# Sink scores in three column tiles, and sink values as a block diagonal

## The chip, the cores and the metric

The kernel runs on one core of one Trainium2 chip. The metric is the time of one execution on the device in microseconds (us); lower is better. Times are medians of several executions. Beside them stands one execution taken with the hardware profiler, from which all rows of the trace come.

## What is computed

Attention with four sink positions and a window of 128, followed by a gated two-layer network:

```python
# q, k, v: 4 batches, 8 heads, 768 positions, 64 wide; n_sink = 4, window = 128
scores = q @ k.transpose(0, 1, 3, 2) / sqrt(64)
rel = pos[:, None] - pos[None, :]
keep = (pos[None, :] < n_sink) | ((rel >= 0) & (rel < window))
a = softmax(where(keep, scores, -1e9))
x = (a @ v).transpose(0, 2, 1, 3).reshape(3072, 512)
# w_in 512 x 2048, w_out 2048 x 512
h = x @ w_in
out = (h * sigmoid(beta * h)) @ w_out
```

All tensors are float32 in memory; the kernel multiplies in bfloat16 and accumulates in float32.

## The kernel before

**Units.** The attention is cut into 32 units. A unit is one batch, one pair of heads and one half of the positions (384 queries); `place(n)` (L441) gives batch, pair, half and buffer. Units 0 to 3 are the first halves of batch 0, 4 to 7 its second halves, and so on, so there are 16 second-half units: 4 to 7, 12 to 15, 20 to 23 and 28 to 31. For each unit q and k are cast to bfloat16 (`cast`, L509, on POOL), turned so that the head dimension lies along the partitions (`transpose_in`, L532, on PE for the first twelve units, a transposing DMA after that), multiplied to scores, sent through the exponential (ACT), masked, multiplied with v (`attend`, L667), divided by the row sums (`normalise`, L702, DVE), and turned back (`transpose_out`, L712) into `xT`, the input of the network.

**Sinks.** Queries of a second half do not see the four sink keys in their window blocks, so these units have a sink part of their own. `sink_keys` (L560, POOL) builds `k_sink`, a 128 by 128 stationary tile that holds the four sink keys of the first head in columns 0 to 3 and of the second head in columns 32 to 35, each zero in the other head's rows; the rest is zero. `scores_sink` (L568) multiplies it with all 384 queries in one matmul (L570) into a bank of PSUM, and one exponential on ACT (L573) writes `E_sink`, 128 by 384. In `attend`, for each of the three blocks of 128 queries, one matmul (L685) multiplies that block of `E_sink` with the unit's part of `v_sink` (130 columns: two heads of 64 values and a one) into the accumulator `av_ps`; the matmuls of the window blocks (L696, 65 columns each) add to it. `v_sink` for all 16 pairs of heads is filled once: `sink_constants` (L428) clears it and sets the ones, two DMAs on ACT's queue (L837) bring the first four rows of v for all heads to `v_rows`, which lies in a part of the buffer `g`, and two casts on DVE (L891) copy them in.

**Pairs of units.** From unit 8 on (`PAIRED`), the scores of two neighbouring units are computed together (`scores_pair`, L620). Scores use the array as two halves of 64 rows, one for each head (L597, L643). The sink scores of a pair's two units are still two matmuls and two exponentials, in the same bank `tr`.

**Network.** `hidden` (L759) multiplies `xT` with w_in in matmuls of 384 columns (L747), `tanh` (L752, ACT) and `gate` (L767, DVE) make `g`, and `project` (L796) multiplies it with w_out in matmuls of 512 columns (L797). The weights come by DMA on SP's queue (`load_w`, L491), in 8 pieces each of w_in and w_out, and are cast by POOL, four of them half by ACT (`cast_w`, L496). Until about 54 us the loads of weights and of q, k and v share the DMA engines.

**Order.** The program is recorded as operations with their reads and writes, in an order set by hand (`EARLY`, `FIRST`, `CASTS`), and `Prog.order` (L182) then lays them on the engines by estimated costs: each engine takes the earliest operation that is ready among the next 160. A node has a flag `tiled`; a change of the flag on PE is reckoned with 97 ns (`CHANGE`). Every engine then runs its list strictly in that order and waits at semaphores.

Of the kernel before, what the change touches and what calls it, by code (L numbers as in the profile page):

```python
# [24 lines left out]
HEAD1 = 32  # L25
# [48 lines left out]
class Node:  # L74
# [5 lines left out]
    def __init__(self, id, eng):  # L80
# [10 lines left out]
        self.tiled = False  # L91


class Prog:
# [39 lines left out]
    def op(self, eng, fn, r=(), w=(), x=(), dma=None, busy=100.0, lag=None, behind=None,  # L134
           give=0.0, line=False, after=None, tiled=False):
# [46 lines left out]
    def order(self):  # L182
# [12 lines left out]
        tiled = False  # L195
# [4 lines left out]
        def best(e):  # L200
# [9 lines left out]
            n = min(c, key=lambda n: (max(n.ready, free[e]) + n.give - self.CHANGE * (tiled and n.tiled), n.id))  # L210
# [97 lines left out]
def bass_streamingllm_window__then__act_swish_beta_kernel(  # L308
# [91 lines left out]
    def constants():  # L400
# [4 lines left out]
        fill("dve", ones[:, :], 1.0, ["ones"], busy=270.0)  # L405
        select(ident[:, :], ones[:, 0:128], [[1, 128]], ALU.is_equal, 0.0, 0, -1, ["ones"], ["ident"])
# [21 lines left out]
    def sink_constants():  # L428
# [131 lines left out]
    def sink_keys(n, after=None):  # L560
        pb = place(n)[3]
        op("gp", lambda e: e.tensor_tensor(
            k_sink[pb][:, 0:2 * HEAD1].rearrange("p (h x) -> p h x", h=2)[:, :, 0:NSINK],
# [4 lines left out]
    def scores_sink(n, bank, name):  # L568
        pb = place(n)[3]
        op("pe", lambda e: e.matmul(bank[:, 0:TT], k_sink[pb][:, :], qkT[pb][:, 1, 0, :],  # L570
                                    start=True, stop=True),
           r=[("k_sink", pb), ("qT", pb, 1)], w=[name], **pe(TT))
        op("act", lambda e: e.activation(E_sink[n % 3][:, :], bank[:, 0:TT], AF.Exp, bias=0.0,  # L573
                                         scale=SCALE),
           x=[name], w=[("E_sink", n % 3)], **act(TT))
# [4 lines left out]
    def scores(n, c, bank, name):  # L580
# [11 lines left out]
        with P.together("pe"):  # L592
            for kb, qb, nq in CHUNKS[half][c]:
                w = 128 * nq
                for hh in range(2):
# [6 lines left out]
                       busy=3.0 + w / 4.8, lag=260.0, tiled=True)  # L602
# [311 lines left out]
    for s in sorted(slots):  # L914
# [16 lines left out]
        for n, step in here:  # L931
# [13 lines left out]
            if step == "av":  # L945
# [107 lines left out]
```

## Time and profile before

| | us |
|---|---|
| median of 3 runs | 222.72 (222.72 to 222.91) |
| profiled execution, its time | 223.15 |
| profiled execution, its span | 221.4 |
| PE busy in the span | 216.1 |
| ACT busy | 145.8 |
| DVE busy | 126.2 |
| POOL busy | 74.0 |

The span reaches from the first to the last instruction; the time has some 1.75 us more around it. PE is TensorE's matmuls, PEld its weight loads, DVE VectorE, ACT ScalarE, POOL GpSimd, SP the queue that issues most DMAs; ACTq is the part of ACT that issues DMAs. Matmuls overlap in the array, so the mean duration of one (327 ns for 384 columns) is longer than the distance between the starts of two; distances are read from groups in the timeline. A busy PE is therefore not the same as a PE at its peak, and the price of a matmul is taken from a dense stretch.

### The profile page before, as it was taken

The numbers are of one execution on the slowest core, as the hardware profiler recorded it, in microseconds if no ns is written. First come the engines' busy times: TensorE is split into PE (matmuls) and PEld (weight loads), VectorE is DVE, ScalarE is ACT, GpSimd is POOL, SyncE is SP. The second block draws the span as 40 slices with busy tenths as digits, with TensorE's granted clock in tenths as the row PEclk, the third lists the DMA queues.
The fourth block names the chain that finished last, engine by engine and source line by source line (L and its number), as shares of the span: only waits on it lengthen the run. The fifth ranks groups of instructions, "written<-read, shape, count | busy, mean of one in ns | idle before, by whom it ended". The sixth has DMA issues, their size and how long they took to land.

```text
span 221.4 us, 4551 instructions
## 1 busy us (share of the span) xinstructions
PE 216.1 (98%) x1765; PEld 123.4 (56%) x1765; DVE 126.2 (57%) x247; ACT 145.8 (66%) x229; POOL 74.0 (33%) x149
## 2 busy tenths in 40 slices
PE   7998999999999999999999999999999999999995
PEld 4554557654555656555465656455656555555543
DVE  5376877773550756665494749484829447074300
ACT  2776997995254868556887778758766675375411
POOL 7697767468625232435012520920000000000000
PEclk9999999999999999999999999999999999999999
DMA  6999999995779994998996989772210202201022
GB/s 192 296 312 345 355 325 266 309 393 146 177 163 236 263 292 117 270 266 134 280 216 140 271 199 224 166 136 60 84 47 18 68 0 83 98 0 47 20 78 96
DMA packets 95438, 39.80 MB, mean 180 GB/s; under 512 B 81960, under 2 KB 88376, under 8 KB 95416
## 3 DMA queue, kind: packets, MB, share of 16 engines
q1 hardware_dynamic: 93760, 38.68, 66.9%
q10 hardware_dynamic: 1656, 0.83, 1.3%
q8 instruction: 14, 0.23, 0.4%
q14 instruction: 8, 0.07, 0.1%
HBM read 27.30 MB, written 6.29 MB: 152 GB/s over the span
## 4 chain that ended last, share of the span: by engine, by line
PE 74%; DMA 11%; SPq 10%; POOL 2%; issue 1%; DVE 0%; POOLq 0%; DVEq 0%
PE acc L797 35%; PE six L747 28%; SPq L467 4%; DMA q_stage<-in_q_dram 4%; SPq L459 4%; PE six L696 4%; PE six L643 4%; DMA wst<-in_moe_w_in_dram 3%; DMA wst<-in_moe_w_out_dram 2%; SPq L493 2%; DMA v_stage<-in_v_dram 1%; PE acc L778 1%; PE six L685 1%; PE six L570 1%; POOL w_out L506 1%
## 5 line engine op out<-in xcount | busy, mean ns | idle before, releaser
L797 PE MATMUL acc<-w_out,g 128*128 128x512 bf16 x368 | 89.2, 379 | 0.2 <-POOL w_out L506 0.2
L755 ACT ACTIVATE th<-six,beta_half 128x384 f32<-128x384 f32 x106 | 61.0, 583 | 26.6 <-PE six L747 21.5
L747 PE MATMUL six<-xT,w_in 128*128 128x384 bf16 x424 | 78.2, 326 | 0.0
L770 DVE SCALAR_TENSOR_TENSOR g<-th,six 128x384 bf16<-128x384 f32 x106 | 57.2, 551 | 25.5 <-ACT th L755 22.9
L747 PEld LDWEIGHTS six<-xT,w_in 128*128 128x128 bf16 x424 | 40.4, 98 | 28.0 <-issue 0.2
L797 PEld LDWEIGHTS acc<-w_out,g 128*128 128x128 bf16 x368 | 34.4, 98 | 37.0 <-issue 1.3
L662 DVE TENSOR_TENSOR E<-E,mask_all 128x1536 bf16<-128x1536 bf16 x24 | 23.9, 998 | 39.6 <-ACT E L654 39.6
L654 ACT ACTIVATE E<-six 128x1536 bf16<-128x1536 f32 x24 | 33.5, 1448 | 15.8 <-PE six L643 15.8
L518 POOL CAST qk<-q_stage 128x384 bf16<-128x384 f32 x32 | 17.6, 552 | 30.1 <-DMA qkT<-qk 15.3
L521 POOL CAST v_aug<-v_stage 128x384 bf16<-128x384 f32 x32 | 17.4, 559 | 18.3 <-DMA v_stage<-in_v_dram 10.9
L805 ACT ACTIVATE out_sb<-acc 128x512 f32<-128x512 f32 x22 | 13.1, 599 | 14.4 <-PE acc L797 14.0
L518 POOL CAST qk<-k_stage 128x384 bf16<-128x384 f32 x31 | 17.4, 564 | 13.0 <-DMA k_stage<-in_k_dram 8.0
L696 PEld LDWEIGHTS six<-v_aug,E 128*128 128x128 bf16 x384 | 17.1, 97 | 3.6 <-DVE E L662 0.3
L696 PE MATMUL six<-v_aug,E 128*128 128x65 bf16 x384 | 18.8, 193 | 0.1
L707 DVE TENSOR_TENSOR o_norm<-six,rden 128x384 bf16<-128x384 f32 x32 | 17.8, 557 | 1.2
L747 PE MATMUL acc<-xT,w_in 128*128 128x384 bf16 x88 | 18.1, 326 | 0.0
L770 DVE SCALAR_TENSOR_TENSOR g<-th,acc 128x384 bf16<-128x384 f32 x22 | 12.0, 551 | 4.0 <-ACT th L755 3.7
L604 ACT ACTIVATE E<-six 128x768 bf16<-128x768 f32 x16 | 12.5, 816 | 2.3 <-PE six L597 2.3
L755 ACT ACTIVATE th<-acc,beta_half 128x384 f32<-128x384 f32 x22 | 12.9, 590 | 1.7 <-PE acc L747 1.4
L747 PEld LDWEIGHTS acc<-xT,w_in 128*128 128x128 bf16 x88 | 7.8, 98 | 4.7 <-DVE g L770 0.4
L643 PEld LDWEIGHTS six<-qkT 64*128 64x128 bf16 x192 | 7.2, 94 | 5.2 <-issue 4.2
L506 POOL CAST w_out<-wst 128x1024 bf16<-128x1024 f32 x8 | 8.3, 1042 | 5.2 <-DMA wst<-in_moe_w_out_dram 5.2
(68 smaller groups left out, 139.2 us busy)
## 6 DMA issues: line engine op xcount, KB each, us to landing
out_dram<-out_sb SPq DMA_DIRECT2D x23, 256.0 KB, 2.5
wst<-in_moe_w_in_dram SPq DMA_DIRECT2D x8, 512.0 KB, 6.9
wst<-in_moe_w_out_dram SPq DMA_DIRECT2D x8, 512.0 KB, 9.2
q_stage<-in_q_dram SPq DMA_DIRECT2D x8, 384.0 KB, 4.7
k_stage<-in_k_dram SPq DMA_DIRECT2D x8, 384.0 KB, 4.0
v_stage<-in_v_dram SPq DMA_DIRECT2D x8, 384.0 KB, 4.3
v_stage<-in_v_dram SPq DMA_DIRECT2D x30, 96.0 KB, 4.4
q_stage<-in_q_dram SPq DMA_DIRECT2D x12, 192.0 KB, 5.1
```

The lines of the kernel that those rows point to most:

```text
L518: op(eng, lambda e, x=x, name=name: e.tensor_copy(qk16[z][:, x, :, :, :], view(name)), r=[(name + "_stage", pb, half, hh) for hh in range( ...
L521: op("gp", lambda e: e.tensor_copy(v_aug[pb][:, 3 * half:3 * half + 3, :, 0:D], view("v")), r=[("v_stage", pb, half, hh) for hh in range(2 ...
L643: pb=pb, half=half: e.matmul(six[:, bank, 128 * at:128 * (at + nq)], qkT[pb][rows, kb // 3, 1, kb % 3 * 128:kb % 3 * 128 + 128], qkT[pb][r ...
L654: op("act", lambda e, u=u, first=first: e.activation(E[u % 2][:, :, :, :].rearrange("p c h x -> p (c h x)"), six[:, first:first + 3, :].re ...
L662: op("dve", lambda e: e.tensor_tensor(both, both, mask_all[:, half, :].unsqueeze(1).to_broadcast([128, 2, 768]), ALU.mult), r=[("E", z, 0) ...
L696: last=(x == len(kbs) - 1): e.matmul(av_ps[:, at + hh * D1:at + hh * D1 + D1], E[z][:, c, h2, col:col + 128], v_aug[pb][:, kb, hh, :], sta ...
L707: op("dve", lambda e: e.tensor_tensor(o_norm[o][:, :, :, :].rearrange("p m h d -> p (m h) d"), src[:, :, 0:D], rden[z][:, :].unsqueeze(2). ...
L747: return op("pe", lambda e: e.matmul(bank, w_in16[:, c, m * 128:(m + 1) * 128], xT[:, c, T * TT:(T + 1) * TT], start=(c == 0), stop=(c == 3)),
L755: op("act", lambda e: e.activation(th[i % 3][:, :], bank, AF.Tanh, bias=0.0, scale=beta_half[:, m:m + 1]), x=[name], r=["beta"], w=[("th", ...
L770: op("dve", lambda e: e.scalar_tensor_tensor(g[T % 2][:, m, :], th[i % 3][:, :], 1.0, bank, ALU.add, ALU.mult), r=[("th", i % 3)], x=[name ...
L797: node = op("pe", lambda e: e.matmul(bank, g[T % 2][:, m, t * 128:(t + 1) * 128], w_out16[:, m, :], start=(m == 0), stop=(m == NM - 1)), r ...
L805: op("act", lambda e: e.activation(out_sb[z][:, :], bank, AF.Copy, bias=0.0, scale=0.5), x=[name], w=[("out_sb", z)], **act(NOUT))
```

## The change

1. **Sink scores in column tiles.** `k_sink` becomes 128 by 32: the four keys of both heads in columns 0 to 7, zeros behind. `scores_sink` issues, for each unit, three matmuls of 128 queries each instead of one of 384. The m-th writes the PSUM partitions 32m to 32m + 31, that is, it uses the m-th strip of 32 columns of the array. For units from 8 on, both units of a pair are in one group of six matmuls, in two stretches of 128 columns of the same bank.
2. **One exponential a pair.** It works on 96 partitions and 256 columns (128 for the single units 4 to 7) and writes `E_sink`, now 128 partitions, two units, 128 columns, in two buffers; the last 32 partitions are cleared once.
3. **Values as a block diagonal.** `v_sink` becomes a tile of one unit, 128 by 6 by 65, in two buffers. Row 32m + 4h + s holds the values of sink s of head h in the columns of block m and head h and zeros elsewhere, so one matmul of 390 columns replaces the three of 130.
4. **Building it.** `v_rows` is a float32 tile of its own, cleared by DVE. The DMAs from v put the rows of both heads in partitions 0 to 7; two more DMAs on ACT's queue copy these to partitions 32 to 39 and 64 to 71 within SBUF, when the first two have landed and the tile is cleared. `own_row`, made by POOL, marks which block and head a row belongs to; for each unit `sink_values` multiplies `v_rows` with it, on DVE for units 4 to 7, on POOL for the others. The call for a unit is recorded behind `attend` of the unit that used the buffer before.
5. **Planner.** The flag `tiled` becomes a number (0 none, 1 rows, 2 columns), and a change between any two is reckoned as before.

In the order that comes out, the operations around these move as well: by the lists of the two programs PE changes between the three shapes 64 times instead of 46, the copies of `v_rows` stand on ACT's queue between the second copy of `qkT` and the exponentials of unit 1, DVE's first `sink_values` stands between the copies L550 and L728 of units 3 and 1, and 18 instead of 19 matmuls of L797 come ahead of the first that needs the last piece of w_out.

```diff
-HEAD1 = 32
+GROUP, ROWS = 32, 2 * NSINK
...
-    v_sink_all = sb("v_sink", (128, NPAIR * 2 * D1), BF16)
-    v_sink = v_sink_all[:, :].rearrange("p (g h e) -> p g h e", g=NPAIR, h=2)
-    k_sink = [sb(f"k_sink{z}", (128, 128), BF16) for z in range(4)]
+    v_rows = sb("v_rows", (128, NPAIR, D), F32)
+    v_sink = [sb(f"v_sink{z}", (128, 6, D1), BF16) for z in range(2)]
+    own_row = sb("own_row", (128, 6), BF16)
+    k_sink = [sb(f"k_sink{z}", (128, GROUP), BF16) for z in range(4)]
...
-    E_sink = [sb(f"E_sink{z}", (128, TT), BF16) for z in range(3)]
+    E_sink = [sb(f"E_sink{z}", (128, 2, 128), BF16) for z in range(2)]
...
+        fill("dve", v_rows[:, :, :], 0.0, ["v_rows"], busy=600.0)
...
-        fill("dve", v_sink_all[:, :].bitcast(F32), 0.0, ["v_sink"], busy=1000.0)
-        fill("dve", v_sink[0:NSINK, :, 0, D:D1], 1.0, ["v_sink"], ["v_sink"], 180.0)
-        fill("dve", v_sink[HEAD1:HEAD1 + NSINK, :, 1, D:D1], 1.0, ["v_sink"], ["v_sink"], 180.0)
+        rows = own_row[:, :].rearrange("p (m h) -> p m h", m=3)
+        select(rows, ones[:, 0:6].rearrange("p (m h) -> p m h", m=3), [[-GROUP, 3], [-NSINK, 2]], ALU.is_ge,
+               0.0, 0, 1, ["ones"], ["own_row"], 150.0)
+        select(rows, rows, [[GROUP, 3], [NSINK, 2]], ALU.is_ge, 0.0, NSINK - 1, -1, ["own_row"],
+               ["own_row"], 150.0)
+        for z in range(2):
+            fill("gp", E_sink[z][:, :, :], 0.0, [("E_sink", z, 0), ("E_sink", z, 1)], busy=150.0)
+            op("gp", lambda e, z=z: e.tensor_copy(v_sink[z][:, :, D:D1], own_row[:, :].unsqueeze(2)),
+               r=["own_row"], w=[("v_sink", z)], busy=100.0)
...
-    def scores_sink(n, bank, name):
-        pb = place(n)[3]
-        op("pe", lambda e: e.matmul(bank[:, 0:TT], k_sink[pb][:, :], qkT[pb][:, 1, 0, :],
-                                    start=True, stop=True),
-           r=[("k_sink", pb), ("qT", pb, 1)], w=[name], **pe(TT))
-        op("act", lambda e: e.activation(E_sink[n % 3][:, :], bank[:, 0:TT], AF.Exp, bias=0.0,
-                                         scale=SCALE),
-           x=[name], w=[("E_sink", n % 3)], **act(TT))
+    def sink_values(n):
+        g = n // 8 * 4 + place(n)[1]
+        op("dve" if n < PAIRED else "gp", lambda e: e.tensor_tensor(
+            v_sink[n % 2][:, :, 0:D], v_rows[:, g, :].unsqueeze(1).to_broadcast([128, 6, D]),
+            own_row[:, :].unsqueeze(2).to_broadcast([128, 6, D]), ALU.mult),
+           r=["v_rows", *(f"v_rows{x}" for x in range(4)), "own_row"], w=[("v_sink", n % 2)],
+           **(dve(480.0) if n < PAIRED else {"busy": 800.0, "lag": 100.0}))
+
+    def scores_sink(units, bank, name):
+        first, z = units[0] % 2, units[0] // 2 % 2
+        with P.together("pe"):
+            for u in units:
+                pb = place(u)[3]
+                for m in range(3):
+                    op("pe", lambda e, u=u, pb=pb, m=m: e.matmul(
+                        bank[GROUP * m:GROUP * m + GROUP, u % 2 * 128:u % 2 * 128 + 128], k_sink[pb][:, :],
+                        qkT[pb][:, 1, 0, 128 * m:128 * m + 128], start=True, stop=True),
+                       r=[("k_sink", pb), ("qT", pb, 1)], w=[name], busy=19.0, lag=260.0, tiled=2)
+        op("act", lambda e: e.activation(
+            E_sink[z][0:3 * GROUP, first:first + len(units), :].rearrange("p u x -> p (u x)"),
+            bank[0:3 * GROUP, 128 * first:128 * (first + len(units))], AF.Exp, bias=0.0, scale=SCALE),
+           x=[name], w=[("E_sink", z, u % 2) for u in units], **act(128 * len(units)))
...
+            if half == 1:
+                op("pe", lambda e: e.matmul(
+                    av_ps[:, 0:6 * D1], E_sink[n // 2 % 2][:, n % 2, :],
+                    v_sink[z][:, :, :].rearrange("p m e -> p (m e)"), start=True, stop=False,
+                    skip_group_check=True),
+                   r=[("E_sink", n // 2 % 2, n % 2), ("v_sink", z)], w=["av"], **pe(6 * D1))
             for mm in range(3):
                 m, at = 3 * half + mm, mm * 2 * D1
-                if half == 1:
-                    op("pe", lambda e, at=at, mm=mm: e.matmul(
-                        av_ps[:, at:at + 2 * D1], E_sink[n % 3][:, mm * 128:mm * 128 + 128],
-                        v_sink[:, n // 8 * 4 + hp, :, :].rearrange("p h e -> p (h e)"),
-                        start=True, stop=False, skip_group_check=True),
-                       r=[("E_sink", n % 3), "v_sink", ("v_sink", 0), ("v_sink", 1)], w=["av"],
-                       **pe(130))
...
     for hh in range(2):
-        rows = slice(HEAD1 * hh, HEAD1 * hh + NSINK)
+        rows = slice(NSINK * hh, NSINK * hh + NSINK)
         s = v[:, :, 0:NSINK, :].rearrange("b (g h) s d -> s h (b g) d", h=2)[:, hh]
-        op("act", lambda e, rows=rows, s=s: e.dma_start(v_rows[rows], s), w=[("v_rows", hh)],
+        op("act", lambda e, rows=rows, s=s: e.dma_start(v_rows[rows], s), r=["v_rows"], w=[f"v_rows{hh}"],
            dma=f"s{hh}", **transfer(1 << 14, 100))
+    for m in (1, 2):
+        op("act", lambda e, m=m: e.dma_start(v_rows[GROUP * m:GROUP * m + ROWS], v_rows[0:ROWS]),
+           r=["v_rows", "v_rows0", "v_rows1"], w=[f"v_rows{m + 1}"], dma=f"s{m + 1}", **transfer(1 << 15, 100))
...
         if n == 2:
-            for hh in range(2):
-                rows = slice(HEAD1 * hh, HEAD1 * hh + NSINK)
-                op("dve", lambda e, hh=hh, rows=rows: e.tensor_copy(v_sink[rows, :, hh, 0:D], v_rows[rows]),
-                   r=[("v_rows", hh), "v_sink"], w=[("v_sink", hh), *wide], after=ended, **dve(600.0))
+            sink_values(4)
+            sink_values(5)
...
+                elif (then := n + (2 if n % 4 < 2 else 6)) < NU:
+                    later.append(lambda then=then: sink_values(then))
```

More of the change, by code (lines that the diff above doesn't have):

```diff
@@ L134, in op @@
     def op(self, eng, fn, r=(), w=(), x=(), dma=None, busy=100.0, lag=None, behind=None,
-           give=0.0, line=False, after=None, tiled=False):
+           give=0.0, line=False, after=None, tiled=0):
         if self.group is not None and self.group.eng == eng:
@@ L209, in best @@
                 return None
-            n = min(c, key=lambda n: (max(n.ready, free[e]) + n.give - self.CHANGE * (tiled and n.tiled), n.id))
+            n = min(c, key=lambda n: (max(n.ready, free[e]) + n.give - self.CHANGE * (tiled > 0 and n.tiled == tiled), n.id))
             start = max(n.ready, free[e] + change(n))
@@ L562, in sink_keys @@
         op("gp", lambda e: e.tensor_tensor(
-            k_sink[pb][:, 0:2 * HEAD1].rearrange("p (h x) -> p h x", h=2)[:, :, 0:NSINK],
+            k_sink[pb][:, 0:ROWS].rearrange("p (h x) -> p h x", h=2),
             qkT[pb][:, 0, 1, 0:NSINK].unsqueeze(1).to_broadcast([128, 2, NSINK]), own_head[:, :, :],
@@ L601, in scores @@
                        r=[("qT", pb, half), ("qkT", pb, kb // 3)], w=[f"{name}{hh}"],
-                       busy=3.0 + w / 4.8, lag=260.0, tiled=True)
+                       busy=3.0 + w / 4.8, lag=260.0, tiled=1)
                 at += w
@@ L648, in scores_pair @@
                    behind=middle.pop(u, None) if (hh, bank) == (1, 1) else None,
-                   busy=27.0 * nq + 1.0, lag=260.0, tiled=True)
+                   busy=27.0 * nq + 1.0, lag=260.0, tiled=1)
                 if (hh, bank) == (0, 1):
```

14 lines of the change are left out of this document (6 added, 8 removed).

## The prediction, made before the changed kernel ran

> **What bounds the kernel now.** I read the page first (busy shares, slices, chain), then the windows by stage, then TensorE's own timeline.
>
> ```profile
> span 221.4 us, 4551 instructions
> PE 216.1 (98%) x1765; PEld 123.4 (56%) x1765; DVE 126.2 (57%) x247; ACT 145.8 (66%) x229; POOL 74.0 (33%) x149
> PE   7998999999999999999999999999999999999995
> ...
> 10.00:15.00 5.00, 4.79 (x63) 2.87 (x61) 2.59 (x8) 3.69 (x7) 4.63 (x10) 1.00 1.02 288
> 15.00:20.00 5.00, 4.48 (x43) 2.61 (x41) 3.19 (x6) 3.05 (x6) 4.42 (x12) 1.00 1.06 346
> 20.00:25.00 5.00, 4.55 (x48) 2.44 (x49) 3.80 (x8) 5.00 (x11) 3.14 (x8) 1.00 1.08 356
> ...
> 60.00:100.00 40.00, 40.00 (x347) 22.44 (x342) 21.68 (x41) 25.84 (x36) 13.31 (x28) 1.00 1.03 228
> 100.00:150.00 50.00, 50.00 (x419) 28.84 (x419) 32.67 (x61) 36.32 (x54) 17.09 (x36) 1.00 0.86 198
> ```
>
> The window columns are the stretch, its length, then busy us (and count) of PE, PEld, DVE, ACT, POOL, then granted clock, DMA share and GB/s. From 60 us on PE has no idle at all at full clock, while ACT, DVE and POOL have 30 to 65% free: there, only the length of PE's own stream counts, and relieving ACT is worth nothing. Before 25 us PE does wait, and DMA and ACT are full. The two are joined at one place:
>
> ```profile
> 48.81 2.54 PE L797 MATMUL acc<-w_out,g 128*128 128x512 bf16 x11
> 51.28 0.83 PE L643 MATMUL six<-qkT 64*128 64x256 bf16 x14
> 52.05 1.90 PE L797 MATMUL acc<-w_out,g 128*128 128x512 bf16 x8
> 54.17 1.25 PE L797 MATMUL acc<-w_out,g 128*128 128x512 bf16 x5 [0.23 <-POOL w_out L506]
> ...
> 53.08 1.04 POOL L506 CAST w_out<-wst 128x1024 bf16<-128x1024 f32 x1 [0.31 <-DMA wst<-in_moe_w_out_dram]
> ...
> 192.06 4.55 PE six L747 x28
> ...
> 207.86 7.55 PE acc L797 x35
> 215.41 2.60 PE acc L778 x16
> 218.01 0.91 PE six L778 x16
> ```
>
> The last four rows give the price of one matmul in a full stream: 512 columns 7.55/35 = 0.216 us, 384 columns 4.55/28 = 0.1625, 128 columns 0.91/16 = 0.057. So the eight matmuls from 52.05 were over at 52.05 + 8 x 0.216 = 53.78, and PE stood until 54.17 for the last piece of w_out, whose cast waits for its transfer. Time won before 54 us is lost in that wait; time lost before it is forgiven up to 0.39 us; what is done behind it counts in full.
>
> **The price of a change of tile shape.** L643 uses the array as two halves of 64 rows. From 48.81, eleven matmuls at 0.216 end at 51.18, but L643 starts at 51.28: 0.10 us to go in. L643's 24 blocks of 128 columns in two halves are 12 x 0.053 (128 columns of the 512 that take 0.216) = 0.64 us and take 0.77 until 52.05: about 0.10 to come out again, and the halves do run side by side. The changed kernel brings a third shape, four column strips of 32. In the order of its instructions PE changes shape 64 times against 46: 6 more before the wait at 54 us (the score groups of units 4 to 7), 12 more behind it (six pair groups, in and out). No row shows a change into column strips; its ends are nothing and the 0.10 of L643. I take 0.10, the nearest row.
>
> By the Trainium skill, TensorEngine Tiling (Array Packing), Key Properties, any change of tiling mode drains the engine; the 0.10 at L643 agrees, and by that rule the column strips pay it too.
>
> **PE's edits, unit by unit** (16 second-half units, 4 early and 12 late):
>
> ```profile
> L570 PE MATMUL six<-qkT,k_sink 128*128 128x384 bf16 x16 | 5.2, 327 | 0.4 <-DVE qkT L550 0.4
> L685 PE MATMUL six<-v_sink,E_sink 128*128 128x130 bf16 x48 | 9.2, 220 | 0.0
> L573 ACT ACTIVATE E_sink<-six 128x384 bf16<-128x384 f32 x16 | 7.9, 492 | 1.8 <-PE six L570 1.8
> ```
>
> Removed: one 384-column score matmul, 0.1625. Added: three of 128 columns. Side by side they cost as little as 0.057, one behind another 3 x 0.057 = 0.171. I take 0.085, nearer the first, because the two halves of L643 overlap almost wholly. Values: three matmuls of 130 columns (3 x 0.057 = 0.171) become one of 390 (0.165): 0.006 won, nearly nothing, as the columns stay.
> - Late, behind the wait: -12 x 0.1625 - 12 x 0.006 + 12 x 0.10 + 12 x 0.085 = -1.95 - 0.07 + 1.20 + 1.02 = +0.20 us; the ends of the tiles give -0.14 and +1.23.
> - Early: -0.65 - 0.02 + 0.60 + 0.34 = +0.27.
>
> The skill speaks against the tiles in one more way: TensorEngine Tiling (Array Packing), Restrictions, says that column tiling switches Fast Weight Load off, and TensorE: Matmul & The Clock Gate, LDWEIGHTS, puts a load at columns/1.2 ns, so 27 ns for 32 columns. Six such loads bare between the tiles of a pair would be 0.16 us, six pairs 1.0 us, an estimate from that page; the late sum would be +1.2 by it, which is where rival 2 ends, and no row here shows whether loads into strips hide.
>
> **ACT and the new copies.** ACT loses 16 exponentials of 0.49 and gets 4 shorter and 6 of 256 columns; late that is worth nothing (above). But two DMAs are added to ACT's queue, the copies of v_rows within SBUF, and they stand between the second copy of qkT and unit 1's exponentials, waiting until v_rows has landed.
>
> ```profile
> 2.92 0.51 ACTq L829 DMA_DIRECT2D beta_stage<-in_moe_beta_dram  x1
> 3.46 0.87 ACTq L837 DMA_DIRECT2D g<-in_v_dram  x2
> 8.25 0.49 ACT L550 COPY qkT<-six 128x384 bf16<-128x384 bf16 x1
> 9.17 1.51 ACT L604 ACTIVATE E<-six 128x768 bf16<-128x768 f32 x2 [0.44 <-PE six L597]
> ...
> beta_stage<-in_moe_beta_dram ACTq DMA_DIRECT2D x1, 8.0 KB, 5.6
> ...
> 18.01 0.34 PE L724 MATMUL six<-ident,o_norm 128*128 128x128 bf16 x3 [0.23 <-DVE o_norm L707]
> 18.35 0.50 PE L747 MATMUL acc<-xT,w_in 128*128 128x384 bf16 x2
> 21.82 0.50 PE L541 MATMUL six<-ident,qk 128*128 128x128 bf16 x6
> 22.37 0.50 PE L589 MATMUL six<-far_b,ident 128*128 128x384 bf16 x2
> ```
>
> beta, issued just ahead on that queue, landed at 2.92 + 5.6 = 8.5; the v_rows loads behind it land between 8.7 and 3.46 + 0.87 + 5.6 = 9.9. I take 9.15. Two issues cost 0.87 (the L837 row; at least half of it). So unit 1's exponentials start at about 10.0 instead of 9.17: +0.85, ends +0.3 and +1.6. Queued behind is the whole chain of units 1 to 3, each unit's exponentials, values and transposes waiting for the one before, down to the transposes at 18.01. There PE has 18.35 - (18.01 + 3 x 0.057) = 0.17 of slack, and at 22.37, where it waits for ACT (22.37 - 21.82 - 6 x 0.057 = 0.21), the shorter exponential of unit 4 gives back some 0.2.
>
> **DVE, POOL, DMA.**
>
> ```profile
> 11.93 0.55 DVE L550 COPY qkT<-acc 128x384 bf16<-128x384 bf16 x1
> 12.95 0.35 DVE L728 COPY xT<-acc 128x384 bf16<-128x384 bf16 x1
> 13.36 0.28 PE L857 MATMUL acc<-ones 128*128 128x256 bf16 x1
> 14.74 1.90 DVE L891 CAST v_sink<-g 4x1024 bf16<-4x1024 f32 x2
> ...
> L707 DVE TENSOR_TENSOR o_norm<-six,rden 128x384 bf16<-128x384 f32 x32 | 17.8, 557 | 1.2
> ```
>
> The two casts of L891 (1.90) go; four multiplies of 384 elements come on DVE, 0.56 each by L707. The first stands between L550 and L728: from 12.48 it ends at 13.04, so L728 is 0.09 late, and PE's filler matmul at 13.36 with unit 2's values behind it as much: +0.1. POOL gets two selects, two fills and two small copies between its first casts (under 1 us, in gaps where it waits for q and k to land) and 12 multiplies at 0.5 to 1 us; from 60 to 150 us POOL is busy 30 of 90 us. A multiply is released by one unit's values and needed by those two units on. Cost nothing; without that cover each would stop PE by its own length. The copies move 64 KB, 0.2 us at the 346 to 356 GB/s of the windows from 15 to 25 us; they could put the last w_out piece off by that much.
>
> **The sum.** Chain before 54 us: 0.85 + 0.1 - 0.17 - 0.2 = 0.58, with about 0.2 of the early PE edits behind 22 us: 0.78. In the new order 18 of L797's matmuls, not 19, stand ahead of the one that needs the last w_out piece: its wait takes 0.39 + 0.22 of a delay, but 0.22 more is done behind it. So the net is the larger of 0.22 and 0.78 - 0.39 = 0.39. With the late +0.20: +0.6 us, a span of 222.0. The profiled execution took 223.15, 1.75 beyond its span, and becomes 223.75; it was 0.43 above the median of 222.72, from which the forecast is 223.3. Its own range is 222.9 to 223.8.
>
> **Rivals.**
> 1. Nothing to be seen: v_rows lands before ACT arrives (+0.3), the delay vanishes in the wait at 54 us (+0.22), and the tiles run fully side by side (-0.14): 222.8. For it: L643's halves. Against: ACT then must not wait for a load at the end of its own queue.
> 2. Tiles one behind another. The matmuls of one unit share all 128 rows; if a strip can't stream while its neighbour does, late +1.23 and early 0.34 more on 0.39: +2.0, 224.7. It decides from 0.07 a unit upwards, where the late sum leaves zero. For it: no row shows column strips overlapping. Against: L643.
> 3. The copies land late. DVE waits for them at 12.48 + 0.85 = 13.3. Issued by 10.0, they are there with the 2.2 us of the early 96 KB loads, but not with the 5.1 of the later ones: 15.1. L728, the filler and unit 2's values queue behind: +1.8, 225.1 at most, 224.2 halfway.
>
> ```profile
> q_stage<-in_q_dram SPq DMA_DIRECT2D x12, 192.0 KB, 5.1
> ...
> k_stage<-in_k_dram SPq DMA_DIRECT2D x8, 96.0 KB, 2.2
> ```
>
> 4. Faster: column strips change shape for nothing, since rows need no regrouping. Late -1.95 - 0.07 + 0.68 = -1.34, early 0.22: -1.1, 221.6. Against: the 0.10 at L643 in both directions.
>
> **How the numbers follow.** Forecast 0.36, rival 1 0.16, rival 2 0.20, rival 3 0.16, rival 4 0.12. A run of this kernel can tell 0.2%, 0.45 us, from no change. Slower: 0.6 of the forecast (its centre lies at +0.6), rivals 2 and 3: 0.58. Same: the rest of the forecast and rival 1: 0.30. Faster: 0.12. The range of 222.2 to 225.1 leaves out rival 4.
>
> **What would show it.** In the changed profile: PE still without idle from 60 us; a gap of some 0.10 us on either side of each group of score tiles, and three starts within a few ns (forecast) or 0.057 apart (rival 2); unit 1's exponentials near 10.0 and the transposes of unit 3's output near 18.8; a shorter wait for the last w_out piece; DVE's first multiply near 13.3 with no wait for a DMA (rival 3 if it has one). The forecast is wrong if PE waits after 60 us for a v_sink from POOL, or if no gap stands at the score groups.

## The result, and the profile after

| | us |
|---|---|
| kernel before, median of 4 runs beside it | 222.78 (222.72 to 222.91) |
| changed kernel, median of 4 runs | 226.47 (226.21 to 226.62) |
| ratio | 1.0164, 95% interval 1.0146 to 1.0181 |
| profiled execution: time, span | 226.21, 224.4 |

The change makes the kernel 3.7 us slower, at a granted clock of 0.99 to 1.00. Some later executions show a lower granted clock, among them the profiled one of no_copies at 0.85; no ratio and no reading of a trace below uses them. The forecast was 223.3, with a range of 222.2 to 225.1: the direction was right, the size was not. The two profiled executions lie closer together, at 223.15 and 226.21 us, so their traces can account for 3.1 of the 3.7 us. The page of the changed kernel, and the first of its windows of the late stretch (columns as before):

```profile
span 224.4 us, 4563 instructions
PE 215.9 (96%) x1765; PEld 120.9 (54%) x1765; DVE 126.8 (57%) x247; ACT 142.6 (64%) x223; POOL 82.9 (37%) x167
PE   7778989999999999999999999999999999999995
...
60.00:100.00 40.00, 40.00 (x362) 22.19 (x361) 23.04 (x44) 25.43 (x35) 19.65 (x36) 1.00 1.03 227
```

PE is busy no longer than before (215.9 against 216.1 us), and from 60 us on it again has no idle. What grew is the idle ahead of that: the first three slices of PE read 7, 7, 7 instead of 7, 9, 9. PE's timeline (start, busy time, line, tiles, count, and in brackets what it waited for) gives the end of the early stretch, a pair's sink group, and the end:

```profile
52.22 2.32 PE L818 MATMUL acc<-w_out,g 128*128 128x512 bf16 x10
54.47 0.83 PE L665 MATMUL six<-qkT 64*128 64x256 bf16 x14
55.24 2.12 PE L818 MATMUL acc<-w_out,g 128*128 128x512 bf16 x9
...
69.58 1.03 PE L818 MATMUL acc<-w_out,g 128*128 128x512 bf16 x4
70.54 0.29 PE L590 MATMUL six<-qkT,k_sink 128*32 128x128 bf16 x6
70.76 1.04 PE L818 MATMUL acc<-w_out,g 128*128 128x512 bf16 x4
```

And PE's last row in its chain of waits:

```profile
220.99 0.91 PE six L799 x16
```

The first pair's scores (now L665, before L643) start at 54.47 instead of 51.28, behind ten matmuls of 512 columns instead of eleven: the chain ahead is 3.19 + 0.22 = 3.41 us later, against the 0.78 of the forecast. The wait for w_out is gone, 0.39 us forgiven as forecast. From that point to PE's end it is 220.99 + 0.91 - 54.47 = 167.43 us, 167.21 without the matmul that changed sides; before it was 218.01 + 0.91 - 51.28 - 0.39 = 167.25. So the late part, forecast at +0.20, is worth -0.04: nothing. The six tiles of a pair take 70.76 - 70.54 = 0.22, of which 0.10 is the change out of the shape, and the way in is 70.54 - 69.58 - 4 x 0.216 = 0.10.

Nearly all of the loss lies before 37 us. PE's waits there, with the transposes of unit 3's output at 19.86, and then the rows of ACT and DVE that make them:

```profile
9.50 0.33 PE L745 MATMUL acc<-ident,o_norm 128*128 128x128 bf16 x3
10.97 0.50 PE L611 MATMUL six<-far_a,ident 128*128 128x384 bf16 x2 [1.14 <-ACT E L626]
...
13.78 0.50 PE L611 MATMUL six<-far_a,ident 128*128 128x384 bf16 x2
15.21 0.28 PE L878 MATMUL acc<-ones 128*128 128x256 bf16 x1 [0.93 <-DVE xT L749]
...
19.86 0.34 PE L745 MATMUL six<-ident,o_norm 128*128 128x128 bf16 x3 [0.23 <-DVE o_norm L728]
...
23.82 0.50 PE L611 MATMUL six<-far_b,ident 128*128 128x384 bf16 x2
...
29.78 0.34 PE L705 MATMUL six<-v_sink,E_sink 128*128 128x390 bf16 x1
30.36 0.54 PE L717 MATMUL six<-v_aug,E 128*128 128x65 bf16 x12 [0.24 <-DVE E L637]
...
32.89 0.34 PE L619 MATMUL six<-qkT 64*128 64x256 bf16 x4
34.05 0.34 PE L619 MATMUL six<-qkT 64*128 64x128 bf16 x4 [0.82 <-DVE qkT L558]
34.31 0.24 PE L590 MATMUL six<-qkT,k_sink 128*32 128x128 bf16 x3
```

```profile
7.62 0.49 ACT L558 COPY qkT<-six 128x384 bf16<-128x384 bf16 x1
8.63 1.42 ACTq L858 DMA_DIRECT2D v_rows<-v_rows  x2
10.10 1.51 ACT L626 ACTIVATE E<-six 128x768 bf16<-128x768 f32 x2 [1.99 <-PE acc L745]
...
14.33 0.56 DVE L578 TENSOR_TENSOR v_sink<-v_rows,own_row 128x384 bf16<-128x384 f32 x1 [0.93 <-DMA v_rows<-v_rows]
...
28.45 0.55 DVE L578 TENSOR_TENSOR v_sink<-v_rows,own_row 128x384 bf16<-128x384 f32 x1
28.91 1.39 DVE L637 TENSOR_TENSOR E<-E,mask_b 128x768 bf16<-128x768 bf16 x1
...
31.84 1.19 DVE L578 TENSOR_TENSOR v_sink<-v_rows,own_row 128x384 bf16<-128x384 f32 x1
```

The chain of waits (start, us, what) has the two DMAs between them:

```profile
4.06 4.49 DMA v_rows<-in_v_dram
...
9.42 4.81 DMA v_rows<-v_rows
```

Three costs can be read (a, b and c below), and the theory to be tested is that they are the loss:
- **a, ACT's queue.** The copy of qkT is done at 7.62 + 0.49 = 8.11, v's first rows land at 4.06 + 4.49 = 8.55, and then ACT spends 1.42 us on the two issues. The row of ACT at 10.10 names a matmul as its releaser, but at 9.50 PE was through with unit 1's scores and turned unit 0's output: what the exponentials waited for is ACT's own queue.
- **b, the landing.** DVE's first multiply stands 0.93 us until the second copy has landed, 4.81 us after its issue. Behind it on DVE is the copy of unit 1's output (L749), for which PE's filler matmul and unit 2's values wait.
- **c, the multiplies of units 6 and 7.** At 28 and 32 us DVE has no idle; the multiplies put off the mask (L637) and a copy of qkT (L558), and two of these operations are stretched, to 1.39 and 1.19 us, where the same forms take 0.55 elsewhere.

The rivals are the score tiles and the order that the planner makes for them, and the loads, which may set that stretch whatever stands ahead of them.

### The profile page after: what moved, and what is told of

Its sections match the earlier page's. It is cut to its first block, busy times and chain, and to the rows that moved or that the text cites. A ratio compares the mean times of both kernels' runs of the same rounds, so it can differ in the third digit from the quotient of the medians.

```text
span 224.4 us, 4563 instructions
## 1 busy us (share of the span) xinstructions
PE 215.9 (96%) x1765; PEld 120.9 (54%) x1765; DVE 126.8 (57%) x247; ACT 142.6 (64%) x223; POOL 82.9 (37%) x167
## 4 chain that ended last, share of the span: by engine, by line
PE 86%; DVE 4%; DMA 4%; ACT 2%; POOL 1%; ACTq 1%; issue 0%; DVEq 0%; POOLq 0%
PE acc L818 36%; PE six L768 30%; PE acc L768 5%; PE six L717 5%; PE six L665 4%; DMA v_rows<-v_rows 2%; DMA v_rows<-in_v_dram 2%; PE acc L799 1%; ACT th L776 1%; PE six L705 1%; ACT E L626 1%; DVE v_sink L578 1%; DVE g L791 1%; DVE qkT L558 1%; PE six L549 1%; DVE o_norm L728 1%
## 5 line engine op out<-in xcount | busy, mean ns | idle before, releaser
L791 DVE SCALAR_TENSOR_TENSOR g<-th,six 128x384 bf16<-128x384 f32 x106 | 56.9, 551 | 28.0 <-ACT th L776 25.6
L818 PEld LDWEIGHTS acc<-w_out,g 128*128 128x128 bf16 x368 | 33.9, 98 | 36.3 <-issue 1.3
L684 DVE TENSOR_TENSOR E<-E,mask_all 128x1536 bf16<-128x1536 bf16 x24 | 23.3, 971 | 38.3 <-ACT E L676 38.3
L578 POOL TENSOR_TENSOR v_sink<-v_rows,own_row 128x384 bf16<-128x384 f32 x12 | 11.4, 948 | 56.5 <-PE six L705 55.4
L526 POOL CAST qk<-q_stage 128x384 bf16<-128x384 f32 x32 | 18.5, 581 | 15.8 <-DMA qkT<-qk 10.4
L529 POOL CAST v_aug<-v_stage 128x384 bf16<-128x384 f32 x32 | 16.5, 531 | 7.5 <-DMA v_stage<-in_v_dram 7.3
L717 PEld LDWEIGHTS six<-v_aug,E 128*128 128x128 bf16 x384 | 15.9, 97 | 5.1 <-DVE E L637 0.5
L728 DVE TENSOR_TENSOR o_norm<-six,rden 128x384 bf16<-128x384 f32 x32 | 17.8, 557 | 1.2
L526 POOL CAST qk<-k_stage 128x384 bf16<-128x384 f32 x31 | 16.6, 540 | 4.8 <-DMA k_stage<-in_k_dram 4.5
L717 PE MATMUL six<-v_aug,E 128*128 128x65 bf16 x384 | 17.1, 193 | 0.3 <-DVE E L637 0.2
L791 DVE SCALAR_TENSOR_TENSOR g<-th,acc 128x384 bf16<-128x384 f32 x22 | 11.9, 550 | 4.1 <-ACT th L776 3.7
L665 PE MATMUL six<-qkT 64*128 64x128 bf16 (+2 forms) x192 | 10.0, 244 | 0.0
```

Source lines behind the costliest of these rows:

```text
L526: op(eng, lambda e, x=x, name=name: e.tensor_copy(qk16[z][:, x, :, :, :], view(name)), r=[(name + "_stage", pb, half, hh) for hh in range( ...
L529: op("gp", lambda e: e.tensor_copy(v_aug[pb][:, 3 * half:3 * half + 3, :, 0:D], view("v")), r=[("v_stage", pb, half, hh) for hh in range(2 ...
L665: pb=pb, half=half: e.matmul(six[:, bank, 128 * at:128 * (at + nq)], qkT[pb][rows, kb // 3, 1, kb % 3 * 128:kb % 3 * 128 + 128], qkT[pb][r ...
L684: op("dve", lambda e: e.tensor_tensor(both, both, mask_all[:, half, :].unsqueeze(1).to_broadcast([128, 2, 768]), ALU.mult), r=[("E", z, 0) ...
L717: last=(x == len(kbs) - 1): e.matmul(av_ps[:, at + hh * D1:at + hh * D1 + D1], E[z][:, c, h2, col:col + 128], v_aug[pb][:, kb, hh, :], sta ...
L728: op("dve", lambda e: e.tensor_tensor(o_norm[o][:, :, :, :].rearrange("p m h d -> p (m h) d"), src[:, :, 0:D], rden[z][:, :].unsqueeze(2). ...
```

## Experiments

Ratios are to the kernel before on the same chip, run beside it. On the chips of the experiments the runs of one kernel lay further apart than in the first result (most of the kernel before between 222.3 and 223.6 us), so the intervals are some 0.25 to 0.6% wide on both sides, and the traces carry as much as the ratios.

**copies_alone.** Only the two copies, put into the kernel before.

```diff
+        fill("dve", v_rows[32:64], 0.0, ["zero"], busy=600.0)
+    for m in (1, 2):
+        op("act", lambda e, m=m: e.dma_start(v_twice[32 * m:32 * m + 8], v_rows[32:40]), ...
```

> The kernel before, with nothing of the change but the two copies within SBUF at the same place of ACT's queue (behind the two loads of v's first rows, ahead of its exponentials), copied to rows that nobody reads, so no engine waits for their landing; DVE also clears 32 rows once at the start, as the copies read them. Theory (ACT waits for the loads, then spends some 1.4 us on two issues, and units 1 to 3 follow late): unit 1's exponentials start 1 to 1.4 us later, of which the slack of 0.17 us at unit 3's transposes and the wait of 0.39 us for the last piece of w_out swallow 0.56: 223.2 to 223.6 us. Rival (the copies' place on ACT costs nothing, the loss is DVE's wait for their landing, or the score tiles): 222.7 to 222.9 us.

Measured: 225.11 us, ratio 1.0069 (1.0038 to 1.0100), more than either side expected. It does not serve as a test: the clearing of 32 rows, among the first things that DVE does, held up its masks, and PE's first work on scores started at 4.20 instead of 3.25 us:

```profile
4.20 0.82 PE L590 MATMUL six<-far_b,ident 128*128 128x384 bf16 x2 [0.81 <-DVE far_b L426]
```

The planner also put the second copy elsewhere, behind the copy of unit 0's output. copies_clean, below, does without both.

**values_later.** Only DVE's two multiplies move; PE, ACT and SP keep their orders.

```diff
-        if n == 2:
-            sink_values(4)
-            sink_values(5)
...
+    turned = transpose_out(3, tr_ps, "tr", "dve")
+    for n in (4, 5):
+        sink_values(n, turned)
```

> The changed kernel, with the multiplies of units 4 and 5 on DVE moved behind the copy of unit 3's transposed output; the orders of PE, ACT and SP stay as they are. Theory (DVE's first multiply stood 0.93 us waiting for the copies to land, and PE's filler matmul and unit 2's values 1.10 us behind it): that gap goes; two multiplies of 0.56 us stand where DVE has 0.6 us idle, which costs up to 0.5 us again. 225.2 to 225.9 us. Rivals (score tiles and shape changes, or ACT's issues alone, set the loss): 226.3 to 226.6 us.

Measured: 225.97 us, 1.0106 (1.0072 to 1.0139), just above what the theory expected, where the kernel before was slower too. DVE waits for no DMA any more, and of PE's gap at 15 us, 15.21 - 13.78 - 2 x 0.1625 = 1.10, only 14.90 - 14.39 - 0.325 = 0.18 is left: b is 0.92 us of the chain. Part of it comes back at 22 us, because the two multiplies, one of them stretched, now stand ahead of unit 4's copy:

```profile
14.39 0.50 PE L611 MATMUL six<-far_a,ident 128*128 128x384 bf16 x2
14.90 0.28 PE L878 MATMUL acc<-ones 128*128 128x256 bf16 x1
...
22.45 0.24 PE L590 MATMUL six<-qkT,k_sink 128*32 128x128 bf16 x3 [0.92 <-DVE qkT L558]
...
20.20 1.32 DVE L578 TENSOR_TENSOR v_sink<-v_rows,own_row 128x384 bf16<-128x384 f32 x2
```

**direct_later.** As values_later, with four loads from HBM in place of the copies.

```diff
+    for m in range(3):
+        for hh in range(2):
+            rows = slice(GROUP * m + NSINK * hh, GROUP * m + NSINK * hh + NSINK)
...
-        op("act", lambda e, m=m: e.dma_start(v_rows[GROUP * m:GROUP * m + ROWS], v_rows[0:ROWS]), ...
```

> As values_later, and the two copies within SBUF are replaced by four more small loads from HBM, straight to rows 32 and 64 on; ACT issues all six at its start, with nothing to wait for, and is done with them before its first exponential. The schedule orders some early PE work in another way for it. Theory (ACT's wait and issues cost about 1 us of the early chain): unit 1's exponentials come 1 to 1.4 us earlier than in the changed kernel, 0.6 to 1.0 us less than values_later: 224.3 to 225.1 us. Rival (ACT's issues cost nothing on the path): as values_later within 0.3 us.

Measured: 225.16 us, 1.0076 (1.0046 to 1.0107), just above the expected range. The transposes of unit 3's output come at 17.95, as early as before the change, but then PE stands for 1.12 us, until 22.42, for a gate of the network, whose weights were late:

```profile
22.42 0.50 PE L768 MATMUL acc<-xT,w_in 128*128 128x384 bf16 x2 [1.12 <-DVE g L791]
...
20.71 0.61 POOL L511 CAST w_in<-wst 128x512 bf16<-128x512 f32 x1 [1.50 <-DMA wst<-in_moe_w_in_dram]
```

In that execution the loads were the wall behind the chain, as the rival named above has it (the loads set that stretch). The early order had changed too, so for a it settles nothing.

**pool67.** The multiplies of units 6 and 7 on POOL.

```diff
-        op("dve" if n < PAIRED else "gp", lambda e: e.tensor_tensor(
+        op("dve" if n < 6 else "gp", lambda e: e.tensor_tensor(
```

> The changed kernel, with the multiplies of units 6 and 7 on POOL instead of DVE, units 4 and 5 as they are; the schedule moves transposes and value groups of these units a little. Theory (the multiplies at 28.45 and 31.84 us hold up DVE's mask and copies, PE waits 0.4 us at 30.4 and 1.0 us at 34.0 for them): some 0.7 to 1.3 us go, less what POOL's casts lose: 225.1 to 225.8 us. Rival (the loss there is a trace of the early delay, or of the order, and not of the multiplies): 226.2 us or more.

Measured: 224.93 us, 1.0085 (1.0052 to 1.0119), a little less than the theory expected. Unit 5's values follow at once, and L619 runs through without its wait of 0.82:

```profile
30.08 0.34 PE L705 MATMUL six<-v_sink,E_sink 128*128 128x390 bf16 x1
30.25 0.53 PE L717 MATMUL six<-v_aug,E 128*128 128x65 bf16 x12
...
32.67 0.57 PE L619 MATMUL six<-qkT 64*128 64x256 bf16 x8
33.18 0.24 PE L590 MATMUL six<-qkT,k_sink 128*32 128x128 bf16 x3
```

What c cost in that execution of the changed kernel follows from the two: (30.36 - 29.78) - (30.25 - 30.08) = 0.41, and (34.31 - 32.89) - (33.18 - 32.67) = 0.91, together 1.3 us.

**no_copies, no67, no_both.** The changed kernel's own order on every engine, with the suspects left out and nothing in their place.

```diff
+            if n.left:
+                continue
...
-           r=["v_rows", "v_rows0", "v_rows1"], w=[f"v_rows{m + 1}"], dma=f"s{m + 1}", ...
+           r=["v_rows", "v_rows0", "v_rows1"], w=[f"v_rows{m + 1}"], dma=f"s{m + 1}", left=True, ...
...
-           r=["v_rows", ...], w=[("v_sink", n % 2)],
+           r=["v_rows", ...], w=[("v_sink", n % 2)], left=n in (6, 7),
```

> The changed kernel in its own order on every engine, with the two copies of v_rows within SBUF left out and nothing in their place (rows 32 and 64 on of v_rows stay zero, so four of each unit's six value blocks lack the sinks). That takes away ACT's wait and issues ahead of unit 1's exponentials and DVE's wait for the landing; the multiplies stay. Theory (these two waits cost 1.3 us at 11 us and 1.1 us at 15 us of PE's stream): PE's gaps there shrink below 0.4 us each, the transposes of unit 3's output come at 17.8 to 18.3 instead of 19.86 us, and the time falls by 1.4 to 2.0 us, since the wait for w_out's last piece or a load of w_in may take some back: a ratio of 1.007 to 1.010 to the kernel before. Rival (the loads of w_in set the stretch behind 18 us anyway, and the copies only fill their wait): the transposes come early, but the ratio stays at 1.013 or more.

Measured: 1.0067 (1.0044 to 1.0090), within what the theory expected and a little better. Where the gaps and the transposes come to lie is not shown by this run.

> The changed kernel in its own order, with DVE's multiplies for units 6 and 7 left out (these two units take the sinks' values of units 4 and 5). Theory (they hold up DVE's mask and copies in its full stretch from 28 to 33 us): PE's gaps of 0.41 us at 30.4 and 0.98 us at 34.0 shrink to 0.2 us or less together, and the time falls by 0.8 to 1.3 us: a ratio of 1.010 to 1.013. Rival (they are only where the early delay shows): the gaps stay, 1.015 to 1.017.

Measured: 1.0100 (1.0073 to 1.0127), as expected. Both of PE's gaps are gone (its timeline there is that of pool67), and the mask is back at 0.55:

```profile
29.95 0.55 DVE L643 TENSOR_TENSOR E<-E,mask_b 128x768 bf16<-128x768 bf16 x1
```

> The changed kernel in its own order, without the copies and without the multiplies of units 6 and 7 (the parts of the computation left out are those of the two runs above). Theory (what the score tiles and the block diagonal do themselves is worth nothing, all of the loss is the copies and these multiplies): the gains add up but for some 0.4 us in the wait for w_out's last piece, a ratio of 1.001 to 1.005. Rival (the score tiles and changes of shape cost more than they save): 1.006 or more, with the first pair of units and the last matmul further apart than in the kernel before.

Measured: 1.0040 (1.0003 to 1.0078), as expected. Taking these parts out removes about three quarters of the loss (1.64 - 0.40 of 1.64%), with the score tiles, the block diagonal and the order untouched; by the interval it is half to nearly all, and two thirds of the 1.23% that after_again, below, shows for the changed kernel. The two gains against the first result, 0.97 and 0.64%, add up to 1.61 and give 1.24 together.

The trace of no_both does not show the early gain. POOL's cast of v began late, after an idle time for which the trace names no cause, and unit 1's exponentials started after 10 us without any copies ahead of them:

```profile
8.13 0.51 POOL L535 CAST v_aug<-v_stage 128x384 bf16<-128x384 f32 x1 [1.33 <-issue]
...
10.22 1.51 ACT L632 ACTIVATE E<-six 128x768 bf16<-128x768 f32 x2 [1.48 <-PE six L625]
```

Unit 3's transposes came at 19.55. This is one of the slower of the 12 executions (225.02 us, median 223.77). Without copies on ACT's queue, unit 1's exponentials start at 10.22 here and at 9.18 in best_a, below: the start of the early stretch moves by some 1 us of itself, and what these runs show of a and b they show by their ratios.

**single.** The price of a change of tile shape: each late unit's tiles in a group of its own.

```diff
-            if step == "sink" and half == 1 and (n < PAIRED or n % 2 == 0):
-                scores_sink((n,) if n < PAIRED else (n, n + 1),
+            if step == "sink" and half == 1:
+                scores_sink((n,),
```

> The changed kernel with the score tiles of each late unit in a group of its own, with an exponential of its own: 12 changes of tile shape more behind 60 us, nothing saved. Theory (a change costs 0.095 us each way, PE's stream alone counts there): 1.1 to 1.2 us more than the changed kernel, a ratio of 1.021 to 1.023. Rival (a change into column tiles is hidden beside other work, and the 0.1 us at them are something else): 1.016 to 1.018.

Measured: 1.0188 (1.0152 to 1.0225), between what the two sides expect, so it alone does not tell them apart. The trace does:

```profile
53.42 0.83 PE L665 MATMUL six<-qkT 64*128 64x256 bf16 x14
...
29.08 0.55 DVE L637 TENSOR_TENSOR E<-E,mask_b 128x768 bf16<-128x768 bf16 x1
```

```profile
221.26 0.91 PE six L799 x16
```

From the first pair, behind ten matmuls again, to the end it is 168.75 us, 1.32 more than in the changed kernel: 0.11 for each of the 12 changes added. In this execution the early stretch lost 1.05 us less (53.42 against 54.47), mostly since the mask and unit 7's multiply were not stretched (0.55 and 0.59 us against 1.39 and 1.19). An early stretch that varies this much hides the price in the whole time.

**copies_clean.** copies_alone without the clearing, 4 rows a copy, and every order as in the kernel before.

```diff
+                x = op("act", lambda e, m=m: e.dma_start(v_twice[32 * m:32 * m + 4], v_rows[32:36]), ...
+                x.behind = P.writer["qkT", 1, 0][0]
```

> The kernel before with every engine's order as it was, and only two copies within SBUF put into ACT's queue behind the second copy of qkT, ahead of unit 1's exponentials: they wait for v's first rows as in the changed kernel, copy 4 rows each to rows that nobody reads until much later, and nothing else changes (no clearing of rows, unlike in copies_alone). Theory (ACT's wait for the loads and its two issues are a cost of their own): unit 1's exponentials start at 10.0 to 10.5 us instead of 9.17, the transposes of unit 3's output 0.7 to 1.2 us later than 18.01, and 0.3 to 0.7 us of it are left behind the wait for w_out: a ratio of 1.0015 to 1.0035. Rival (the copies cost only through DVE's wait for their landing): 0.999 to 1.001.

Measured: 223.63 us, 1.0043 (1.0018 to 1.0069). ACT and PE:

```profile
8.53 1.34 ACTq L897 DMA_DIRECT2D g<-g  x2
9.92 1.51 ACT L611 ACTIVATE E<-six 128x768 bf16<-128x768 f32 x2 [1.14 <-PE six L604]
...
18.75 0.34 PE L731 MATMUL six<-ident,o_norm 128*128 128x128 bf16 x3 [0.23 <-DVE o_norm L714]
```

Unit 1's exponentials start 0.75 us late and unit 3's transposes 0.74 (18.75 against 18.01). So a costs by itself, with no multiply waiting for the copies: it is about 0.7 us of the chain. At PE's end this trace has 0.17 us of it left (its last row starts at 218.18 instead of 218.01), since the wait for w_out took the rest. The ratio is more than that, and why is not shown.

**after_again, later_pool67, best_a.** The changed kernel once more, and its repairs step by step. best_a moves the copies to SP:

```diff
     load_w(2)
+    for m in (1, 2):
+        op("sp", lambda e, m=m: e.dma_start(v_rows[GROUP * m:GROUP * m + ROWS], v_rows[0:ROWS]), ...
     load(5)
```

> The changed kernel as it is, beside the others on the same chip: 1.015 to 1.018, and the two gaps of 1.1 to 1.3 us at 11 and 15 us again.

Measured: 225.96 us, 1.0123 (1.0088 to 1.0159), less than expected, though the interval reaches 1.015, with both gaps again (1.04 and 0.87 us of waiting at 11.31 and 15.50). At the multiplies of units 6 and 7 this execution lost less than the first one: (30.65 - 30.07) - 0.17 = 0.41 and (34.05 - 33.18) - 0.51 = 0.36, together 0.8 us.

> The changed kernel with the multiplies of units 4 and 5 moved behind the copy of unit 3's output (values_later) and those of units 6 and 7 on POOL (pool67). Theory (DVE's wait for the landing and the multiplies in its full stretch are two separate costs): the two gains add up, and what is left is ACT's wait and issues: a ratio of 1.003 to 1.007. Rival (both runs won the same time, set in truth by the loads of w_in): no better than pool67 alone, 1.008 or more.

Measured: 224.44 us, 1.0069 (1.0043 to 1.0095). It is better than either part, but not clearly so; the interval reaches to the rival.

> As later_pool67, and the two copies within SBUF are issued by SP, behind the third piece of w_in, where v's first rows have long landed, instead of ACT. Theory (ACT's wait and issues are the third cost): unit 1's exponentials start at 9.0 to 9.3 us, and the ratio is 0.999 to 1.003, about that of the kernel before, since the late part gains nothing. Rival (SP's queue and the DMA engines set the stretch behind 18 us, and two issues more there put off unit 5's loads by 1 us): 1.004 or more.

Measured: 224.43 us, 1.0060 (1.0032 to 1.0089): missed. Its trace up to unit 3 is that of the kernel before to 0.01 us (exponentials at 9.18, transposes at 18.01), so a and b are gone. Then the two multiplies stand ahead of unit 4's copy:

```profile
18.01 0.34 PE L745 MATMUL six<-ident,o_norm 128*128 128x128 bf16 x3 [0.23 <-DVE o_norm L728]
...
21.08 0.24 PE L590 MATMUL six<-qkT,k_sink 128*32 128x128 bf16 x3 [1.09 <-DVE qkT L558]
...
18.72 1.44 DVE L578 TENSOR_TENSOR v_sink<-v_rows,own_row 128x384 bf16<-128x384 f32 x2
```

**best_e, best_b.** What remained: unit 5's multiply later on DVE (best_e), or all four on POOL (best_b).

```diff
-    for n in (4, 5):
-        sink_values(n, turned)
+    sink_values(4, turned)
...
+            if (n, step) == (5, 'a'):
+                later.append(lambda done=done: sink_values(5, done))
```

> As best_a, but only unit 4's multiply stands on DVE between the copy of unit 3's output and that of unit 4's q and k; unit 5's comes after the copy of unit 5's q and k, where DVE had 0.7 us idle before. Theory (what best_a still lost at 21 us are the two multiplies ahead of unit 4's copy, 1.26 us of waiting instead of 0.57): that gap is back at 0.6 to 0.8 us, unit 4's values start at 24.3 to 24.7 instead of 25.15 us, a ratio of 1.001 to 1.004. Rival (the rest is the score tiles, their changes of shape and the new order, or the loads): the gap shrinks but the ratio stays at 1.005 or more.

> As best_a, but the multiplies of units 4 and 5 are on POOL as well, so DVE has none. Theory (DVE's multiplies are the cost): DVE's copy of unit 4's q and k no longer waits behind them, PE's gap at 21 us is back at 0.57 us: a ratio of 1.000 to 1.004. Rival (POOL's casts of q, k and w_in are on the path between 20 and 30 us, and two multiplies of 0.83 us ahead of them cost as much): 1.005 or more.

Measured: best_e 224.62 us, 1.0082 (1.0052 to 1.0113); best_b 224.97 us, 1.0113 (1.0048 to 1.0178). Both missed. In best_e's profiled execution PE waited 1.58 us at 20.43 for a cast of w_in. In best_b unit 4's values even start at 23.78, earlier than the 24.22 before the change, and then PE waits again:

```profile
23.78 0.33 PE L705 MATMUL six<-v_sink,E_sink 128*128 128x390 bf16 x1
...
26.22 0.34 PE L745 MATMUL six<-ident,o_norm 128*128 128x128 bf16 x3 [0.65 <-DVE qkT L558]
```

Between 18 and 35 us DVE, POOL, ACT and the loads all stand close to the path, and the planner orders them anew with each edit; a repair of one wait moved it to another. The last 0.6% or so is not settled. No version tried is faster than the kernel before.

## Why the prediction was wrong

- **What bounds the kernel, the wait at 54 us, PE without idle from 60 us:** right. The wait took 0.39 and no more.
- **A change of shape costs 0.10 each way, into column strips too:** right, by 0.10 at a pair's group and 0.11 in `single`. Rival 4 falls.
- **Score tiles:** 0.085 a unit was taken; two units take 0.22 - 0.10 = 0.12, so 0.06 each, the end at 0.057. They run side by side, rival 2 falls, and the late sum is -0.04 instead of +0.20. By the rules of the Trainium skill on column tiling and weight loads that the prediction weighed (TensorEngine Tiling (Array Packing), Restrictions; TensorE: Matmul & The Clock Gate, LDWEIGHTS) six bare loads would have cost 0.16 a pair, an estimate. The trace does not show them: the six tiles and the change out take 0.22 together.
- **ACT's queue (a):** the mechanism and place were right, +0.85 forecast, 0.74 in copies_clean and 10.10 - 9.17 = 0.93 in the changed kernel. That the size fits is in part luck. The rows landed at 8.55 and not 9.15, but two issues of such copies take 1.34 to 1.42 us, not 0.87; and in this execution unit 0's exponentials had begun 0.62 us early (6.23 instead of 6.85). In after_again they began at 6.85, and unit 1's came at 10.45, 1.28 late.
- **The copies' landing (b), the first step that failed.** "+0.1" was put on DVE's first multiply, and its wait kept as rival 3 at 0.16 with 1.8 us at most. It happened, and cost 0.92. DVE's first multiply came at 14.33 with a wait, not at 13.3 without, and unit 3's transposes at 19.86, not 18.8. The copies took 4.8 us to land, near the 5.1 of the later loads, with the loads of q, k and v under way.
- **The multiplies of units 6 and 7 (c), the second step that failed.** "Cost nothing" was argued for POOL's twelve, from POOL's idle time; of DVE's four only the first was placed in its timeline. Those at 28.45 and 31.84 fall where DVE has no idle and cost PE 1.3 us; no67 and pool67 show it. Without them (no67, 1.0100, on the first result's scale 225.0 us) the time is just inside the range. The size goes by the execution: with the same order it is 0.8 us in after_again and 0.2 in `single`, by how far POOL's casts stretch these operations.
- **The sum.** In the changed kernel's trace a and b are 0.93 + 0.92 = 1.85 us, which is how late unit 3's transposes come (19.86 against 18.01). At 23.82, where it was 22.37 before, 1.45 is left: the forecast's two credits, 0.17 and 0.2, came in. With c's 1.3 and the 0.27 estimated for PE's early edits, 3.0 of the 3.41 us by which the chain is late are named; where the other 0.4 arises is not shown. 0.39 and 0.04 are won back behind, which leaves the 3.0 us by which the spans differ. That the copies and the multiplies of units 6 and 7 are most of the loss is shown by the ratio of no_both. The split among a, b and c is that of one execution.

## What to carry to other kernels

An operation that is hidden must be placed in the timeline of its own engine, each instance by itself: of four multiplies of 0.56 us, two cost next to nothing by their own length, and two cost PE 0.4 and 0.9 us in the profiled execution, by where they fell. A DMA that waits can cost three times, as it did here: its wait (0.5 us) and its issue (1.42 us) stop the issuing engine's own work, and the first reader waits for the landing, here 4.8 us after the issue, which is near the longer of the two durations that the prediction had from the trace. When a saving and its price are both on the busiest engine, work out the net first: here three tiles won 0.10 a unit and the changes of shape gave it all back, so there was nothing to pay the set-up with.

## What the runs showed of the hardware

Operations of DVE with two inputs in SBUF were stretched when a cast of POOL had begun first. In the changed kernel, POOL's row beside the mask and the multiply shown above:

```profile
28.84 1.05 POOL L514 CAST w_in<-wst 128x1024 bf16<-128x1024 f32 x1 [0.75 <-DMA wst<-in_moe_w_in_dram]
31.59 1.04 POOL L514 CAST w_in<-wst 128x1024 bf16<-128x1024 f32 x1 [1.69 <-DMA wst<-in_moe_w_in_dram]
```

The mask at 28.91, begun 0.07 us behind the cast, took 1.39, the multiply at 31.84 took 1.19; without a POOL instruction beside them these forms took 0.55 to 0.56 in the runs here. The gate (L791), which reads one input from PSUM, kept its 0.55. The Trainium skill has the rule (SBUF — State Buffer, Who interferes with whom): a DVE instruction with two SBUF inputs and a POOL instruction that reads SBUF exclude each other, and whichever starts first holds the port for its whole length. The two rows agree: the mask lost 0.84 us while the cast had 0.98 to go. In `single` the mask began at 29.08, ahead of POOL's first cast, and kept its 0.55, while the two casts took longer than 1.05 each:

```profile
29.26 2.32 POOL L514 CAST w_in<-wst 128x1024 bf16<-128x1024 f32 x2 [0.80 <-DMA wst<-in_moe_w_in_dram]
```

The prediction had looked for contention only in DMA.

A copy within SBUF of 8 rows by 4 KB took ACT 0.64 to 0.75 us to issue, and one of 4 rows not much less (1.34 us for two), where two loads of 16 KB from HBM took the same queue 0.87 us.
